# Spectral mixing with three complex products in place of four, an inverse transform in 64-row tiles, and part of the weight conversion on GpSimd

## The chip, the cores and the metric

The kernel runs on one core of a Trainium2 chip. The metric is the device time of one execution in microseconds (us). The engines have short names: PE is TensorE (PEld its weight loads), DVE is VectorE, ACT is ScalarE, POOL is GpSimd, and SP is SyncE, which issues nearly all transfers.

## The reference

A spectral layer is followed by two MLPs. B is 2, S 3008, D 256, the hidden width 2048.

```python
X = np.fft.rfft(x, axis=1)
Yr = Xr @ w_r - Xi @ w_i + b_r
Yi = Xr @ w_i + Xi @ w_r + b_i
Yr = np.sign(Yr) * np.maximum(np.abs(Yr) - 0.01, 0.0)      # the same for Yi
y = np.fft.irfft(Yr + 1j * Yi, n=S, axis=1)
h = y @ w_in;  g = np.maximum(h, 0) + alpha * np.minimum(h, 0);  y = g @ w_out
h = y @ w_in2; g = np.where(h >= 1, h, np.where(h <= -1, 0, (h + 1)**2 / 4)); out = g @ w_out2
```

The MLP weights are float64 and come to the chip as pairs of 32-bit words.

## The kernel before

The program is written in order by hand: each engine works through its instructions in the order of the code, and semaphores tie them together.

1. **First transform.** `f1(g)`, 16 groups: four products of 256 columns each, whose results are written to memory (`store_a`) and read back in another layout (`load_a` into `a_sb`).
2. **Mixing loop.** 24 items `(b, i)`, 12 for each batch entry. `f2` makes the spectrum of an item with four products of 128 columns. ACT and DVE split it into a high part `xh` and a low part `xl` with the imaginary part negated beside it. `mix` multiplies by the two weight matrices `wm`: each output half takes six kinds of products (high and low of the data with high and low of the weights) over two halves of the depth, 24 products of 256 columns in all. DVE adds the bias and shrinks (`y32`). `i1` is the first step of the inverse transform, two float32 products of 256 columns. In round `j` of the loop stand `f2` of item j+2, `mix` of item j and `i1` of item j-2.
3. **Conversion of the first MLP's weights.** `conversions` is a generator that turns 16 blocks (`f`) of word pairs into a high and a low part. Each block takes four steps: `begin_w` (ACT) with the previous block's `fraction_w`; `words_w` (ACT, DVE) with the previous block's `high_w` (ACT); `low_w`; then `clamp_w` and `sign_w`. The mixing loop and the MLP loop each advance it by some steps in every round. When it has ended, the MLP loop advances `second_weights`, the second MLP's weights, in the same way.
4. **Second inverse step** `p3`, with operands of 48 rows in 64-row halves and results of 64 rows, run in pairs (`p3_two`) in rounds 17, 19 and 21.
5. **The MLPs.** `trio` takes 48 steps, with `first` and `second` of six products of 512 columns each, then further chunks and pairs of chunks.

Where PE waits for a bank of its result memory (PSUM), the bank's tag tells who holds it: `e` and `h` have two buffers each, `o0` to `o3` one each.

Of the kernel before, what the change touches and what calls it, by code (L numbers as in the profile page):

```python
# [31 lines left out]
def fourier_constants():  # L32
# [21 lines left out]
    for k in range(NK):  # L54
# [39 lines left out]
def spectral_mlp_kernel(ctx: ExitStack, tc: tile.TileContext, x, w_r, w_i, bias, c_f1, c_f2,  # L94
# [55 lines left out]


# [33 lines left out]
    def clamp_w(m):  # L185
        V.tensor_scalar(m, m, W_MAX, W_MIN, op0=ALU.min, op1=ALU.max)

    def conversions(l, fs):
# [5 lines left out]
        for k in range(n + 1):  # L194
# [139 lines left out]
    ps = psum.tile([128, 256], F32, tag="h", name="ps_warm")
    for _ in range(3):
        T.matmul(ps, warm[:, 0:128], warm, start=True, stop=True)


    c47 = base.tile([96, 96], F32, name="c47")
# [87 lines left out]
    wm = [block(f"c{k}", [128, 2, 2, D], F32R, f"wm{k}") for k in range(2)]  # L427
    held = []
    for g in range(8, 16):
        f1(g, held if g == 15 else None)  # L430
        if g < 15:
            store_a(g, 0)
        if g in (13, 14):

            hi, lo = (wm[g - 13][:, z].rearrange("p c (h q) -> p c q h", h=2) for z in range(2))
# [579 lines left out]
```

## Time and profile before

| | us |
|---|---|
| median of 3 runs (1104.27 to 1104.53) | 1104.45 |
| the profiled execution | 1104.76 |
| its span in the profile | 1103.0 |
| PE, DVE, ACT, POOL busy | 1094.4, 914.4, 863.6, 0.2 |
| mixing loop, from its first product to the second MLP step | 34.85 to 150.18 |
| the 48 `trio` steps, about | 146 to 269 |

Busy time of PE is a model of pipelined products, so the pace of PE is read from the starts of its instructions, not from how long each is said to take. Start times are us from the start of the span. A product of two float32 operands shows as two records, one of two float32r operands as one.

### The profile page before, as it was taken

The page shows a single profiled execution, that of the slowest core. Times are in us where ns is not written, and L with a number is a line of the kernel's source. Part 1 is how long each engine was busy: PE and PEld are TensorE (multiplying, and loading weights), DVE is VectorE, ACT ScalarE, POOL GpSimd, SP SyncE. Part 2 cuts the span into 40 slices and gives each one's busy share as a digit, 9 for nine tenths or more (in the row PEclk, how much of TensorE's full clock was granted, in tenths as well). Part 3 has the DMA queues.
Part 4 walks back from the last instruction along what each step waited for, and adds up shares of the span by engine and source line. Part 5 has one row for each costly group of instructions (what it writes and reads, how often), then busy time and mean ns, then how long its engine had stood idle before and what let it go on. Part 6 is the DMA issues. An engine that isn't in the chain of part 4 may idle for free.

```text
span 1103.0 us, 17331 instructions
## 1 busy us (share of the span) xinstructions
PE 1094.4 (99%) x6416; PEld 969.4 (88%) x6416; DVE 914.4 (83%) x1578; ACT 863.6 (78%) x1636; POOL 0.2 (0%) x4
## 2 busy tenths in 40 slices
PE   9999999999999999999999999999999999999998
PEld 7999988888888998888889988888899888888897
DVE  3579968888778989999999999877878878878876
ACT  3555678878777889999989978877778878877876
POOL 0000000000000000000000000000000000000000
PEclk9999999999999999999999999999999999999999
DMA  9997663101322403323235623010010000100101
GB/s 288 305 285 252 185 168 82 32 1 58 111 101 96 153 21 115 115 81 111 96 136 189 218 107 135 1 39 1 1 39 1 37 1 1 39 1 1 39 1 37
DMA packets 50004, 101.34 MB, mean 92 GB/s; under 512 B 5024, under 2 KB 27392, under 8 KB 49920
## 3 DMA queue, kind: packets, MB, share of 16 engines
q1 hardware_dynamic: 49664, 100.08, 27.8%
q8 instruction: 51, 0.84, 0.3%
q14 instruction: 33, 0.27, 0.1%
q10 hardware_dynamic: 256, 0.16, 0.0%
HBM read 64.70 MB, written 35.52 MB: 91 GB/s over the span
## 4 chain that ended last, share of the span: by engine, by line
PE 83%; ACT 8%; DVE 7%; issue 2%; ACTq 0%; DVEq 0%
PE pq L114 9%; PE pq L115 9%; PE pq L113 9%; PE psm L467 6%; PE seeded L113 3%; PE psh L113 3%; PE psh L115 3%; PE psh L114 3%; PE pso L113 3%; PE pso L114 3%; PE seeded L114 3%; PE seeded L115 3%; PE pso L115 3%; PE ps L387 3%; PE psA L113 2%; PE psA L115 2%
## 5 line engine op out<-in xcount | busy, mean ns | idle before, releaser
L113 PE MATMUL pq<-gh,w 128*128 128x512 f32 (+1 forms) x576 | 216.7, 376 | 0.8 <-ACT yt L802 0.4
L114 PE MATMUL pq<-gl,w 128*128 128x512 f32 (+1 forms) x576 | 216.5, 376 | 0.8 <-DVE gl L773 0.6
L115 PE MATMUL pq<-gh,w 128*128 128x512 f32 (+1 forms) x576 | 215.8, 375 | 0.0
L770 ACT ACTIVATE gh<-ta 128x512 fp32r<-128x512 f32 (+1 forms) x144 | 88.6, 627 | 90.8 <-DVE ta L767 86.0
L113 PEld LDWEIGHTS pq<-gh,w 128*128 128x128 f32 x576 | 108.8, 189 | 16.3 <-ACT yt L802 2.1
L114 PEld LDWEIGHTS pq<-gl,w 128*128 128x128 f32 x576 | 108.8, 189 | 15.6 <-DVE gl L773 2.8
L115 PEld LDWEIGHTS pq<-gh,w 128*128 128x128 f32 x576 | 108.9, 189 | 12.7
L773 DVE TENSOR_TENSOR gl<-tb,gh 128x512 fp32r<-128x512 f32 (+1 forms) x96 | 65.3, 680 | 55.9 <-ACT gh L770 55.6
L773 DVE TENSOR_TENSOR gl<-ta,gh 128x512 fp32r<-128x512 f32 (+1 forms) x144 | 97.5, 677 | 3.9 <-ACT gh L770 2.0
L110 DVE TENSOR_TENSOR gl<-ta,gh 128x512 fp32r<-128x512 f32 (+1 forms) x96 | 65.1, 678 | 42.8 <-ACT gh L107 42.6
L578 ACT ACTIVATE ta<-psh 128x512 f32<-128x512 f32 (+1 forms) x96 | 56.7, 591 | 50.2 <-DVE gl L110 32.7
L861 DVE TENSOR_TENSOR h<-psC,s 128x512 f32<-128x512 f32 (+1 forms) x72 | 48.9, 680 | 29.7 <-PE psC L115 25.9
L113 PE MATMUL psh<-mxh,w 128*128 128x512 f32 (+1 forms) x192 | 72.4, 377 | 0.5 <-ACT tb L579 0.5
L114 PE MATMUL pso<-gl,w 128*128 128x512 f32 (+1 forms) x192 | 72.4, 377 | 0.0
L113 PE MATMUL pso<-gh,w 128*128 128x512 f32 (+1 forms) x192 | 72.3, 377 | 0.0
L114 PE MATMUL psh<-mxl,w 128*128 128x512 f32 (+1 forms) x192 | 71.9, 375 | 0.0
L115 PE MATMUL pso<-gh,w 128*128 128x512 f32 (+1 forms) x192 | 71.9, 375 | 0.0
L115 PE MATMUL psh<-mxh,w 128*128 128x512 f32 (+1 forms) x192 | 71.9, 375 | 0.0
L581 DVE SCALAR_TENSOR_TENSOR ta<-ta,nalpha,tb 128x512 f32<-128x512 f32 (+1 forms) x96 | 70.5, 734 | 0.0
L767 DVE SCALAR_TENSOR_TENSOR tb<-tb,h 128x512 f32<-128x512 f32 (+1 forms) x96 | 60.6, 673 | 0.0
L107 ACT ACTIVATE gh<-ta 128x512 fp32r<-128x512 f32 (+1 forms) x96 | 60.2, 628 | 0.3 <-DVE ta L581 0.3
L770 ACT ACTIVATE gh<-tb 128x512 fp32r<-128x512 f32 (+1 forms) x96 | 59.2, 617 | 1.6 <-DVE tb L767 1.6
(141 smaller groups left out, 2723.4 us busy)
## 6 DMA issues: line engine op xcount, KB each, us to landing
s<-kept SPq DMA_DIRECT2D x32, 512.0 KB, 4.0
u<-in_w_in SPq DMA_DIRECT2D x32, 256.0 KB, 3.6
u<-in_w_out SPq DMA_DIRECT2D x32, 256.0 KB, 3.7
kept<-sh SPq DMA_DIRECT2D x16, 512.0 KB, 2.9
kept<-wh SPq DMA_DIRECT2D x16, 512.0 KB, 3.0
w<-kept SPq DMA_DIRECT2D x16, 512.0 KB, 4.7
v_dr<-ve SPq DMA_DIRECT2D x12, 512.0 KB, 3.6
v<-v_dr SPq DMA_DIRECT2D x32, 192.0 KB, 5.1
```

Of the source, the lines that this page charges most:

```text
L107: A.activation(hi, src, AF.Copy)
L110: V.tensor_tensor(lo, src, hi.bitcast(F32), op=ALU.subtract)
L113: T.matmul(ps, wl, xh, start=start, stop=False, skip_group_check=chained)
L114: T.matmul(ps, wh, xl, start=False, stop=False, skip_group_check=chained)
L115: T.matmul(ps, wh, xh, start=False, stop=stop, skip_group_check=chained)
L467: T.matmul(o, x[:, 2 * k + c, off:off + 128], wm[r][:, z, c, :].rearrange("p (h q) -> p q h", h=2), start=n == c == 0, stop=n == 5 and c == 1)
L578: A.activation(ta, ps, AF.Relu, scale=-1.0)
L581: V.scalar_tensor_tensor(ta, ta, nalpha[:, f:f + 1], tb, op0=ALU.mult, op1=ALU.add)
L767: V.scalar_tensor_tensor(self.t, self.t, 1.0, self.h, op0=ALU.min, op1=ALU.max)
L770: A.activation(halves(self.gh, self.m), like_halves(self.t, self.m), AF.Copy)
L773: V.tensor_tensor(halves(self.gl, self.m), like_halves(self.t, self.m), halves(self.gh, self.m).bitcast(F32), op=ALU.subtract)
L861: V.tensor_tensor(blk.h, ps[x], ps[y_], op=ALU.add)
```

## The change

- The complex product uses three real ones. `f2` lays its result out as real, imaginary and their sum; `mix_sum` multiplies the sum by `w_r`, DVE adds the bias and writes the result twice into one of two fixed banks (`ri`), and `mix` lets PE add two further products to what stands there. Each of the three takes six products of 256 columns (high by low, high by high, low by high over two halves of the depth). `wm` holds `w_r`, `-(w_r + w_i)` and `w_i - w_r`.
- The shrinking is an ACT `Relu` and one DVE instruction.
- `i1` takes four products with 64 rows of depth in place of two with 128; even and odd ones use the lower and the upper rows and write different banks.
- For `f < 7`, `clamp_w`, the product in `fraction_w` and both instructions of `low_w` run on GpSimd.
- In the loops, rounds 5 to 22 advance the conversion by 1 or 2 steps in turn (2 before, with 2 more in round 17); `trio` advances it by 1 step from step 2 on and by 2 in every third step below 38 (1 before, from step 5, none in every eighth).
- At the start, the last two groups of the first transform stand behind the first `f2`, and their inputs are loaded behind the first `load_a`. `p3` runs singly in rounds 16 to 21.

```diff
@@ conversion
+    NG = 7
+    def side(f):
+        return G if f < NG else V
...
         V.tensor_scalar(p.bitcast(U32), m.bitcast(U32), 0xFF800000, None, op0=ALU.bitwise_and)
-        V.tensor_tensor(p, p, u[:, :, 0].bitcast(F32), op=ALU.mult)
+        side(f).tensor_tensor(p, p, u[:, :, 0].bitcast(F32), op=ALU.mult)
...
-        V.tensor_tensor(m, m, wt[l, f][:, 0, :].bitcast(F32), op=ALU.subtract)
-        V.tensor_tensor(wt[l, f][:, 1, :], m, p, op=ALU.add)
+        side(f).tensor_tensor(m, m, wt[l, f][:, 0, :].bitcast(F32), op=ALU.subtract)
+        side(f).tensor_tensor(wt[l, f][:, 1, :], m, p, op=ALU.add)
...
-                clamp_w(live[l, fs[k]][1])
+                clamp_w(live[l, fs[k]][1], side(fs[k]))
@@ start
     for g in range(8):
         f1(g)
         store_a(g, 0)
-        load_x(8 + g)
+        if g < 6:
+            load_x(8 + g)
...
     load_a(0, A_PARTS[:2])
+    load_x(14)
+    load_x(15)
...
+        if g == 12:
+            split_wm(0, wm32[0])
+            ws = [rot.tile([128, 2, D], F32, tag=t, name=f"ws{t}") for t in ("cm", "cp")]
+            V.scalar_tensor_tensor(ws[0], wm32[0], -1.0, wm32[1], op0=ALU.mult, op1=ALU.subtract)
+            V.tensor_tensor(ws[1], wm32[1], wm32[0], op=ALU.subtract)
+            split_wm(1, ws[0])
+        if g == 13:
+            split_wm(2, ws[1])
+    for k in range(2):
+        f2(*items[k], **(dict(tag="e") if k else dict(tag="o3", bufs=1)))
+        f1(14 + k)
+        store_a(14 + k, 0)
+    mix_sum(*items[0])
@@ f2
-        A.activation(xh[:, :, 64:192], ps, AF.Copy)
-        A.mul(xh[:, :, 0:64], ps[:, :, 64:128], -1.0)
-        V.tensor_tensor(xl[:, :, 64:192], ps, xh[:, :, 64:192].bitcast(F32), op=ALU.subtract)
-        A.mul(xl[:, :, 0:64], xl[:, :, 128:192].bitcast(F32), -1.0)
+        A.activation(xi, ps[:, 256:512], AF.Copy)
+        V.tensor_tensor(s32, ps[:, 0:256], xi, op=ALU.add)
+        A.activation(xh[:, 0:512], ps, AF.Copy)
+        A.activation(xh[:, 512:768], s32, AF.Copy)
+        V.tensor_tensor(xl[:, 0:512], ps, xh[:, 0:512].bitcast(F32), op=ALU.subtract)
+        V.tensor_tensor(xl[:, 512:768], s32, xh[:, 512:768].bitcast(F32), op=ALU.subtract)
@@ mix
+    def product3(o, x, t, w, start):
+        o = o.rearrange("p (q h) -> p q h", h=2)
+        for n, (z, v) in enumerate(((0, 1), (0, 0), (1, 0))):
+            for c in range(2):
+                T.matmul(o, x[z][:, t, c, :], w[:, v, c, :].rearrange("p (h q) -> p q h", h=2),
+                         start=start and n == c == 0, stop=n == 2 and c == 1, skip_group_check=not start)
...
+    def mix_sum(b, i):
+        ps = psum.tile([128, 1, D], F32, tag="o2", bufs=1, name=f"psk{b}_{i}")
+        product3(ps[:, 0, :], xt[b, i], 2, wm[0], True)
+        V.tensor_tensor(ri[i % 2], ps.to_broadcast([128, 2, D]), b_t, op=ALU.add)
...
-            for n, (r, x, z) in enumerate(((0, xh, 1), (0, xh, 0), (1, xh, 1), (1, xh, 0), (0, xl, 0), (1, xl, 0))):
-                for c in range(2):
-                    off = 0 if r else 64
-                    T.matmul(o, x[:, 2 * k + c, off:off + 128], wm[r][:, z, c, :].rearrange("p (h q) -> p q h", h=2),
-                             start=n == c == 0, stop=n == 5 and c == 1)
...
-        V.tensor_tensor(t, ps, b_t.to_broadcast([128, 2, D]), op=ALU.add)
-        V.tensor_scalar(cl_, t, LAM, -LAM, op0=ALU.min, op1=ALU.max)
-        V.tensor_tensor(y32, t, cl_, op=ALU.subtract)
+        x, y = xt.pop((b, i)), ri[i % 2]
+        for z in range(2):
+            product3(y[:, z, :], x, 1 - z, wm[1 + z], False)
+        A.activation(t, y, AF.Relu, bias=-LAM)
+        V.scalar_tensor_tensor(y32, y, LAM, t, op0=ALU.add, op1=ALU.min)
@@ i1
-        for k in range(2):
-            T.matmul(ps[:, k, :], n_t[i // 4][:, (2 * i + k) % 8, :], y32[:, k, :], start=True, stop=True)
+        for z in range(2):
+            for k in range(2):
+                rows = slice(64 * k, 64 * k + 64)
+                n = 2 * (i % 4) + z
+                T.matmul(ps[k], n_t[i // 4][rows, n, :], y32[rows, z, :], start=z == 0, stop=z == 1)
...
-        A.activation(ve[b][:, 2 * (i % 2):2 * (i % 2) + 2, :], ps, AF.Copy)
+        for k in range(2):
+            A.activation(ve[b][:, 2 * (i % 2) + k, :], ps[k], AF.Copy)
@@ loops
-        if 0 < j < n - 2:
+        if j < n - 2:
             f2(*items[j + 2])
+        if j + 1 < n:
+            mix_sum(*items[j + 1])
         mix(*items[j])
...
-        if j in (17, 19, 21):
-            p3_two(j - 17)
+        if 16 <= j < 22:
+            p3(j - 16)
...
-        for _ in range(j == 2 or (2 if 5 <= j < n - 1 else 0) + (2 if j == 17 else 0)):
+        for _ in range(j == 2 or (1 + j % 2 if 5 <= j < n - 1 else 0)):
             next(conv)
...
-        if 5 <= i < len(trio) and i % 8 != 0 and next(conv, more) is more:
-            next(more, None)
+        if 2 <= i < len(trio):
+            for _ in range(1 + (i % 3 == 0 and i < 38)):
+                if next(conv, more) is more:
+                    next(more, None)
```

PE in one round of the mixing loop, before: `psf` is written by `f2`, `psm` by `mix`, `psi` by `i1`; `fh` and `fl` are `xh` and `xl`.

```order
L447 MATMUL psf_9_693<-m_102,a_210 128x128 x4
L467 MATMUL psm_7_704<-wm_237,fh_7_581 128x256 x4
L467 MATMUL psm_7_704<-wm_238,fh_7_581 128x256 x4
L467 MATMUL psm_7_704<-wm_237,fl_7_582 128x256 x2
L467 MATMUL psm_7_704<-wm_238,fl_7_582 128x256 x2
...
L481 MATMUL psi_5_735<-y_0_5_614,n_104 128x256 x2
```

The same place of the changed kernel; `psk` is written by `mix_sum`, and `ri` by `mix`.

```order
L440 MATMUL psf_8_645<-m_102,a_204 128x2x64 x4
L461 MATMUL psk_7_659<-wm_235,fh_7_592 128x256 x4
L461 MATMUL psk_7_659<-wm_235,fl_7_593 128x256 x2
L461 MATMUL ri_77<-wm_236,fh_6_545 128x256 x4
L461 MATMUL ri_77<-wm_236,fl_6_546 128x256 x2
L461 MATMUL ri_77<-wm_237,fh_6_545 128x256 x4
L461 MATMUL ri_77<-wm_237,fl_6_546 128x256 x2
L514 MATMUL psi_4_0_683<-y_0_4_575,n_104 128x256
L514 MATMUL psi_4_1_684<-y_0_4_575,n_104 128x256
L514 MATMUL psi_4_0_683<-y_0_4_575,n_104 128x256
L514 MATMUL psi_4_1_684<-y_0_4_575,n_104 128x256
```

Of the 24 products for `psm` (the left-out rows are the second output half), 18 are left, six of them for the item that follows, and `i1` has four products where it had two.

ACT in one round of the mixing loop in which the conversion stands, before: `ve` is what `i1` gave, `cm`, `u` and `w` belong to the conversion, and the rows behind them are the next item's.

```order
L484 ACTIVATE ve_6_794<-psi_7_845 128x512
L162 ACTIVATE u_2_631<-u_2_631 128x512
L183 ACTIVATE w_1_856<-cm_1_690 128x512
L452 ACTIVATE fh_0_868<-psf_0_863 128x4x128
L453 ACTIVATE fh_0_868<-psf_0_863 128x4x64
L455 ACTIVATE fl_0_869<-fl_0_869 128x4x64
```

ACT in round 7 of the changed kernel; `t` is the `Relu`, and `s` the copy of the imaginary part or the sum beside it.

```order
L501 ACTIVATE t_7_733<-ri_78 128x512
L518 ACTIVATE ve_4_689<-psi_5_0_737 128x256
L518 ACTIVATE ve_4_689<-psi_5_1_738 128x256
L163 ACTIVATE cm_1_748<-u_1_482 128x512
L168 ACTIVATE u_1_482<-u_1_482 128x512
L189 ACTIVATE w_0_753<-cm_0_637 128x512
L448 ACTIVATE s_0_10_765<-psf_10_758 128x256
L450 ACTIVATE fh_10_763<-psf_10_758 128x512
L451 ACTIVATE fh_10_763<-s_0_10_765 128x256
```

An item has six instructions on ACT where it had four, and in such a round three of the conversion's stand ahead of the next item's first.

PE at the start of the mixing loop, before; `ps_1_7` is the last group of the first transform.

```order
L387 MATMUL ps_1_7_0_309<-x_7_206,c_81 96x256 x2
L387 MATMUL ps_1_7_1_312<-x_7_206,c_81 96x256 x2
L447 MATMUL psf_315<-m_100,a_210 128x128 x4
L447 MATMUL psf_329<-m_100,a_210 128x128 x4
L467 MATMUL psm_0_340<-wm_237,fh_0_320 128x256 x4
```

The same in the changed kernel:

```order
L440 MATMUL psf_0_305<-m_100,a_204 128x2x64 x4
L393 MATMUL ps_1_6_0_319<-x_6_207,c_81 96x256 x2
L393 MATMUL ps_1_6_1_323<-x_6_207,c_81 96x256 x2
L440 MATMUL psf_1_328<-m_100,a_204 128x2x64 x4
L393 MATMUL ps_1_7_0_342<-x_7_209,c_81 96x256 x2
L393 MATMUL ps_1_7_1_346<-x_7_209,c_81 96x256 x2
L461 MATMUL psk_0_351<-wm_235,fh_0_310 128x256 x4
```

Two groups of the first transform moved behind the first `f2`.

## Rows read from the trace of the kernel before

**Rows 1.** The page's first part: busy us, share of the span, instructions.

```profile
PE 1094.4 (99%) x6416; PEld 969.4 (88%) x6416; DVE 914.4 (83%) x1578; ACT 863.6 (78%) x1636; POOL 0.2 (0%) x4
```

**Rows 2.** Timeline, PE, one round of mixing: start, us, engine, line, operation.

```profile
47.10 1.05 PE L447 MATMUL psf<-m,a 128*128 128x128 f32 x8
47.91 1.14 PE L467 MATMUL psm<-wm,fh 128*128 128x256 f32 x8
...
50.67 1.03 PE L481 MATMUL psi<-y,n 128*128 128x256 f32 x4
...
51.54 1.05 PE L447 MATMUL psf<-m,a 128*128 128x128 f32 x8
```

**Rows 3.** Stretches: length, busy PE, PEld, DVE, ACT, POOL, PEclk, DMA share, GB/s.

```profile
46.89:77.90 31.01, 31.01 (x253) 30.31 (x252) 22.43 (x39) 15.34 (x32) 0.00 (x0) 1.00 0.92 302
90.00:100.00 10.00, 10.00 (x82) 9.74 (x82) 9.63 (x19) 6.32 (x14) 0.00 (x0) 1.00 0.52 188
156.00:270.00 114.00, 114.00 (x530) 99.82 (x529) 95.46 (x162) 88.74 (x161) 0.00 (x0) 1.00 0.22 54
```

**Rows 4.** Timeline, PE, around a `p3_two` (L549) in the mixing loop.

```profile
112.78 1.03 PE L481 MATMUL psi<-y,n 128*128 128x256 f32 x4
113.74 2.09 PE L549 MATMUL ps<-g,v 48*64 48x47 f32 x128
115.77 1.16 PE L447 MATMUL psf<-m,a 128*128 128x128 f32 x8
116.68 1.14 PE L467 MATMUL psm<-wm,fh 128*128 128x256 f32 x8
```

**Rows 5.** Groups, 0 to 330 us: busy us, mean ns; idle before, releaser.

```profile
L454 DVE TENSOR_TENSOR fl<-psf,fh 128x512 fp32r<-128x512 f32 x24 | 16.5, 687 | 7.5 <-ACT fh L453 7.5
L452 ACT ACTIVATE fh<-psf 128x512 fp32r<-128x512 f32 x24 | 14.3, 597 | 2.0 <-PE psf L447 2.0
L453 ACT ACTIVATE fh<-psf 128x256 fp32r<-128x256 f32 x24 | 9.3, 388 | 0.0
L266 DVE TENSOR_TENSOR sh<-w 128x256 f32<-128x256 f32 x16 | 6.0, 418 | 0.0
```

**Rows 6.** The same view: the conversion's instructions, one of each for a block.

```profile
L162 ACT ACTIVATE u<-u 128x512 f32<-128x512 uint32 x16 | 13.5, 845 | 0.0
L157 ACT ACTIVATE cm<-u 128x512 f32<-128x512 f32 x16 | 13.1, 818 | 4.3 <-DMA u<-in_w_out 2.8 <-DVE w L179 1.5
L174 DVE TENSOR_TENSOR cp<-cp,u 128x512 f32<-128x512 f32 x16 | 12.4, 773 | 0.6
L168 DVE SCALAR_TENSOR_TENSOR cm<-cm,cp 128x512 uint32<-128x512 uint32 x16 | 11.1, 692 | 0.5
L179 DVE TENSOR_TENSOR w<-cm,cp 128x512 fp32r<-128x512 f32 x16 | 11.1, 692 | 0.5
L178 DVE TENSOR_TENSOR cm<-cm,w 128x512 f32<-128x512 f32 x16 | 11.0, 688 | 1.7 <-ACT w L183 1.6
L183 ACT ACTIVATE w<-cm 128x512 fp32r<-128x512 f32 x16 | 10.2, 640 | 0.1
L163 DVE TENSOR_SCALAR cp<-u 128x512 uint32<-128x512 uint32 x16 | 7.5, 468 | 0.0
L173 DVE TENSOR_SCALAR cp<-cm 128x512 uint32<-128x512 uint32 x16 | 6.8, 424 | 0.3
L186 DVE TENSOR_SCALAR cm<-cm 128x512 f32<-128x512 f32 x16 | 6.7, 420 | 0.0
```

**Rows 7.** Timeline: the first `f2`'s weight load; the second `load_a`; `f2` of item 12.

```profile
33.01 1.86 PEld L447 LDWEIGHTS psf<-m,a 128*128 128x128 f32 x16 [0.16 <-DMA a<-a_dr]
...
71.10 0.82 SPq L361 DMA_DIRECT2D a<-a_dr  x2
...
78.16 1.05 PE L447 MATMUL psf<-m,a 128*128 128x128 f32 x8
```

**Rows 8.** Transfers by line, the `load_a` parts of 256 KB: median us to landing.

```profile
a<-a_dr SPq DMA_DIRECT2D x8, 256.0 KB, 4.2
```

More of the change, by code (lines that the diff above doesn't have):

```diff
@@ L183, in high_w, with clamp_w @@
         A.activation(wt[l, f][:, 0, :], m, AF.Copy)
-    def clamp_w(m):
-        V.tensor_scalar(m, m, W_MAX, W_MIN, op0=ALU.min, op1=ALU.max)
+    def clamp_w(m, engine=V):
+        engine.tensor_scalar(m, m, W_MAX, W_MIN, op0=ALU.min, op1=ALU.max)
     def conversions(l, fs):
@@ L322, in second_weights @@
         yield
-    turn = [0]
+    turn = [2]
     def obank(shape, name, ahead=None):
@@ L330, in obank @@
         return psum.tile(shape, F32, tag=f"o{k}", bufs=1, name=name)
-    warm = rot.tile([128, 256], F32, tag="ta", name="warm")
+    warm = rot.tile([128, 512], F32, tag="ta", name="warm")
     V.memset(warm, 0.0)
[L334 to L339, printed above, removed]
+    ri = [psum.tile([128, 2, D], F32, tag=f"o{k}", bufs=1, name=f"ri{k}") for k in range(2)]
+    for k in range(2):
+        T.matmul(ri[k].rearrange("p z e -> p (z e)"), warm[:, 0:128], warm, start=True, stop=True)
+    c47 = block("small", [128, 128], F32, "c47")[0:96, 0:96]
     A.dma_start(c47, c_f1)
@@ L426, in spectral_mlp_kernel, with f2 @@
     next(conv)
[L427 to L435, printed above, removed]
-            split(wm32[g - 13].rearrange("p c (q h) -> p c q h", h=2), hi, lo, A)
     items = [(b, i) for b in range(B) for i in range(NK // 2)]
     xt, y_32, ve = {}, {}, {}
-    def f2(b, i, ps=None):
-        if ps is None:
-            ps = psum.tile([128, 4, 128], F32, tag="h", name=f"psf{b}_{i}")
+    def f2(b, i, **where):
+        ps = psum.tile([128, 2, 2, 2, R2], F32, **(where or {"tag": "h"}), name=f"psf{b}_{i}")
         for k in range(2):
             for c in range(2):
-                T.matmul(ps[:, 2 * k + c, :], a_sb[b][:, 2 * i + k, c * 128:(c + 1) * 128],
+                T.matmul(ps[:, :, c, k, :], a_sb[b][:, 2 * i + k, c * 128:(c + 1) * 128],
                          m_t[i // 4][:, (2 * i + k) % 8, :], start=True, stop=True)
@@ new lines, in mix_sum, with split_wm @@
+    def mix_sum(b, i):
+        ps = psum.tile([128, 1, D], F32, tag="o2", bufs=1, name=f"psk{b}_{i}")
+        product3(ps[:, 0, :], xt[b, i], 2, wm[0], True)
+        V.tensor_tensor(ri[i % 2], ps.to_broadcast([128, 2, D]), b_t, op=ALU.add)
+    def split_wm(k, w):
+        hi, lo = (wm[k][:, z].rearrange("p c (h q) -> p c q h", h=2) for z in range(2))
+        split(w.rearrange("p c (q h) -> p c q h", h=2), hi, lo, A)
+    for g in range(8, 14):
+        f1(g)
+        store_a(g, 0)
+        if g == 12:
[6 more added lines that the diff above has]
+            split_wm(2, ws[1])
@@ L605, in p3_two @@
                 load_v(k)
-    for j in range(2):
-        f2(*items[j], obank([128, 4, 128], f"psf_{j}", 2 + j))
-        if j == 0:
-            for (dst, ps), copy in zip(held, (lambda d, p: A.activation(d, p, AF.Copy), V.tensor_copy)):
-                copy(dst, ps)
-            store_a(15, 0)
     for j in range(n):
-        if 0 < j < n - 2:
+        if j < n - 2:
             f2(*items[j + 2])
+        if j + 1 < n:
+            mix_sum(*items[j + 1])
         mix(*items[j])
-        if j == 0:
-            f2(*items[2])
         if j >= 2:
```

42 lines of the change are left out of this document (22 added, 20 removed).

## The prediction

> **What bounds the kernel now.** I read the busy times first: PE is busy for 99% of the span, DVE for 83%, ACT for 78%, and GpSimd does nothing [rows 1]. Since PE's busy time is a model, I checked it in the timeline of one round of the mixing loop [rows 2]. `f2` starts at 47.10, `mix` at 47.91, `i1` at 50.67 and the next `f2` at 51.54. So a round takes 4.44 us, made of 0.81 for `f2`, 2.76 for `mix` and 0.87 for `i1`, and one part starts where the last one's work ends. The 24 products of `mix` take 2.76 / 24 = 0.115 us each. The stretches say the same: 82 PE records in 10 us, and 253 in 31 [rows 3], are the 36 records of a round every 4.4 us. PE sets the pace, and what is taken from its queue is won unless another engine becomes late. The one that is near is DVE: 9.63 us of 10 while the conversion stands beside the mixing, with ACT at 6.32 [rows 3]. In the MLP steps PE issues 530 records in 114 us, 2.58 us for a step of twelve, with DVE at 95.46 of 114 us, or 2.16 a step, and ACT at 88.74, or 2.01 [rows 3]. The granted clock is 1.00 in all these stretches.
>
> **Mixing: what goes.** Six of 24 products leave each item: 6 x 0.115 = 0.69 us, and over 24 items 16.6 us.
>
> **Mixing: `i1` in row halves.** It has four products where it had two, each with the same 256 columns. If the lower and the upper rows work side by side it still takes 0.87 us; one after the other it takes 1.74. No row shows this shape. The nearest is `p3_two`, which uses 64-row halves and results of 64 rows: 128 records of 47 columns between 113.74 and 115.77, 15.9 ns each [rows 4]. `f2` takes 0.81 / 8 = 101 ns for a record of 128 columns [rows 2], so 47 columns alone would take 37 ns. `p3_two` is 2.3 times as fast. The two halves of its result can give at most a factor of 2, so at least 1.17 comes from the row halves. That bounds `i1` between 0.87 and 1.74 / 1.17 = 1.49 us. I take 0.87: at 15.9 ns for a load and a product `p3_two` may be held by issuing alone, and `i1` has 109 ns for each of its eight records.
>
> **Mixing: the seams.** Going from full height to halves costs something. From `i1` to `p3_two` it is 112.78 to 113.74, 0.96 where `i1` takes 0.87; the `f2` behind it takes 115.77 to 116.68, 0.91 for 0.81 [rows 4]. That is 0.19 us for both seams, paid once for each item now: 24 x 0.19 = 4.6 us. The lower bound is nothing, should the seams hide behind loads. `p3` run singly borders on `i1`, so its seams about cancel against those of the three pairs it replaces. A round is then 4.44 - 0.69 + 0.19 = 3.94 us.
>
> **DVE and ACT in the mixing.** DVE's item is a sum and a split of 256 columns (0.418 each), a split of 512 (0.687), the bias and the shrinking (like that split): 2.90 us [rows 5]. A block's conversion costs DVE 4.16 us in seven instructions, of which the four that move to GpSimd are 0.420 + 0.773 + 0.688 + 0.692 = 2.57 and the three that stay 1.58 [rows 6]. At 1.5 of four steps a round that is 0.59, so DVE needs 3.49 of 3.94 us. The 28 conversion steps of the loop reach just through the seven blocks that GpSimd serves. ACT's item is three copies of 256 columns at 0.388 (the imaginary part and two halves of `i1`'s result), one more for the sum, and two instructions of 512 at 0.597, the `Relu` among them: 2.75 us [rows 5]. A block's three ACT instructions are 0.845 + 0.818 + 0.640 = 2.30 [rows 6], so ACT needs 2.75 + 0.86 = 3.61 of 3.94, up from 63% to 92%. On average both fit. In single rounds they don't: in rounds 7 and 15 all three conversion instructions stand in front of the next item's first copy, in round 5 two (1.66), in rounds 10 and 13 two (1.49). What is queued behind them is the chain imaginary copy, split, copy of the sum, low part, bias (0.39 + 0.60 + 0.39 + 0.42 + 0.69 = 2.49). It begins 0.78 after the round's start, when `i1`'s copies are done, and has to end when the next `mix_sum` wants bank `o2`, 3.94 + 0.81 = 4.75 after it. The room is 1.48 us. Rounds 5, 7 and 15 exceed it by 0.18, 0.82 and 0.82, 1.8 in all; if the hand-overs between engines take 0.5 of it, the sum with rounds 10 and 13 is 4.3. I take 3.0; rounds 16 to 21 have `p3`'s 1.0 us as cover. Lower bound 0, if the pieces one item ahead absorb it.
>
> **GpSimd.** Its 28 instructions are costed at nothing, because `clamp_w` waits only on ACT's first instruction and `low_w` only on ACT's high part, both given a round or so earlier, and a block has 2.7 rounds, 10 us. No row shows GpSimd arithmetic; the price without cover stands under the rivals.
>
> **The start.** Before, the first `f2` waited 0.16 us for `load_a` at 33.01 [rows 7], so transfer and PE arrive together. Now PE comes there two groups of the first transform earlier, 8 products of 256 columns or 4 x 0.87 = 3.5 us. The transfer gets ahead by two input groups of 393 KB, which at 302 GB/s [rows 3] is 2.6 us. So some 0.9 us of waiting is new. DVE also has a third split and two sums of the mixing weights, 2 us and more, in front of the first item. I take 1.5 us of loss, from 0 to 3.5.
>
> **Item 12.** The next batch entry's `load_a` is issued at 71.10 [rows 7] and lands 4.2 us later [rows 8], at 75.3; transfers fill 0.92 of the time until then [rows 3], so I don't expect it sooner. Its `f2` stood at 78.16 [rows 7]. Now ten rounds give back 6.9, eight pairs of seams take 1.5, the start 1.5 and rounds 5 and 7 some 1.5: 75.8. No wait is added, but the loop can't be over 2.9 us ahead there, which caps the gain.
>
> **MLP steps.** The loop leaves 39 conversion steps to `trio` where it left 28, and nine more steps of the second weights come forward: 20 steps at 4.16 / 4 = 1.04, the conversion's price for both, are 20.8 us of DVE over 48 steps, 0.43 each. DVE goes from 2.16 to 2.59 us against PE's 2.58: full, not yet over. ACT goes to about 2.25. I take 1.0 us, from 0 to 3.
>
> **Sum.** -16.6 + 4.6 + 3.0 + 1.5 + 1.0 = -6.5 us. From the profiled execution's 1104.76 that gives 1098.3; the median stands 0.3 below it, so 1098.0.
>
> **Rivals.** *Row halves one after the other (slower).* `i1` then takes 0.87 us more, 24 x 0.87 = 20.9, of which the 3.0 for ACT would be hidden: 1098 + 17.9 = 1116. It turns slower than before from 0.4 us an item on. Against it speaks the factor of 2.3 [rows 4]; for it, that only 1.17 of it is proved for rows.
>
> *GpSimd holds up DVE.* If each of the 28 instructions stopped DVE for as long as DVE itself takes for one (0.69 [rows 6]), DVE would lose 19.3 us in rounds 5 to 22. Its room there is 18 x 0.45 and 6 x 1.0 of `p3`, 14; the other 5 come back to PE: 1103, no change. It would be slower from about 0.8 us a stop on. Rows can't decide it, but most of DVE's instructions in the mixing read one operand from PSUM, and many will not meet GpSimd.
>
> The Trainium skill has a rule for this ("SBUF — State Buffer", section "SBUF: two separate sides"): VectorE and GpSimd share a port pair by an exclusive lock held for a whole instruction, and VectorE needs it in its 2-port modes or with two SBUF inputs. Its "GPSIMD Engine Reference" (section 3.1) gives about 2.6 cycles at 1.2 GHz for each element of a two-input instruction, so I estimate 1.1 us for one of ours. If every one were a stop, 31 us, the time by these pages would be near 1115. No row of this trace shows GpSimd working, so it stays a rival.
>
> *The items' chain sets the pace.* If the chain over ACT and DVE holds all rounds near 4.3 us instead of 3.94, 24 x 0.36 = 8.6 are gone instead of the 3.0: 1103.6, no change. For it: ACT at 92%.
>
> *More than forecast.* Seams hidden and no burst felt: 2.9 us by item 12 and 14 x 0.69 = 9.7 behind it: 1092.
>
> **How the numbers follow.** The measurement tells 0.2%, 2.2 us, from no change. The forecast (1094.5 to 1102) gets 0.60, more than it 0.15, rows in turn 0.06, GpSimd 0.11 (half of it slower), the chain 0.05, others on the slow side 0.03. So faster 0.76, same 0.10, slower 0.14. The range runs from 1092, the capped best case, to 1105, which leaves out the slow cases.
>
> **What would show it.** The round on PE falls from 4.44 to near 3.94 us, with `i1` at 0.87 plus seams; `i1` at 1.5 or more proves the first rival. PE waits on the bias or on the low parts in rounds 7 and 15. GpSimd's instructions should stand beside DVE's without stretching them. In the MLP steps 2.58 us a step shows that DVE still keeps up. The forecast fails if a step's new cost on DVE or ACT shows as PE idle over several rounds.

## The result and the profile after

The changed kernel takes 1120.1 us (median of 4 runs, 1119.43 to 1121.5), the kernel before beside it 1104.49. The ratio is 1.0142, with a 95% interval of 1.0124 to 1.0159: slower by 1.4%, where 1098.0 was forecast and the range ended at 1105. The profiled execution took 1121.5 us, its span 1119.3.

The page's first part of the changed kernel, which answers to [rows 1]:

```profile
PE 1096.9 (98%) x6366; PEld 953.6 (85%) x6366; DVE 911.1 (81%) x1577; ACT 884.1 (79%) x1685; POOL 33.5 (3%) x32
```

PE is not busy for less time than before, though it has 144 products less, and the span is 16.3 us longer. So time went in idle stretches and in slow ones. Where, shows when the same work is reached. Five marks divide the span: `f2` of item 4 on PE (the mixing loop at `j` = 2), and ACT's `tb<-psh`, its second copy of a step's `first`, of the MLP steps 0, 48 (the first behind `trio`), 60 and 95. The table gives the time to the first mark and from each to the next, from the starts of these rows, for every run below. All later comparisons come from it.

| run | to item 4 | mixing | `trio` | steps 48 to 60 | steps 60 to 95 | rest |
|---|---|---|---|---|---|---|
| before | 42.7 | 105.5 | 123.3 | 35.5 | 93.9 | 702.1 |
| after | 52.8 | 102.8 | 129.5 | 41.4 | 92.9 | 700.0 |
| e1_start | 51.8 | 103.2 | 129.6 | 41.2 | 92.8 | 700.0 |
| e2_even | 50.4 | 103.3 | 132.4 | 35.7 | 93.6 | 702.0 |
| e3_dve | 50.8 | 105.9 | 129.1 | 41.4 | 92.9 | 699.9 |
| e5_three | 51.5 | 101.8 | 131.3 | 35.1 | 94.0 | 702.4 |
| e6_loads | 48.1 | 103.2 | 129.6 | 41.2 | 92.9 | 700.0 |
| e7_sched | 50.3 | 108.7 | 124.7 | 35.5 | 94.0 | 702.0 |
| e8_two | 49.3 | 110.0 | 124.7 | 35.6 | 93.8 | 702.0 |
| e9_rows | 50.8 | 112.0 | 130.0 | 41.3 | 93.0 | 700.0 |
| e10_mend | 49.9 | 101.8 | 131.2 | 35.2 | 93.9 | 702.0 |
| e11_mend_gp | 48.1 | 101.8 | 141.6 | 35.9 | 93.6 | 702.1 |
| e12_thin_after | 51.4 | 100.2 | 126.3 | 41.3 | 92.7 | 699.9 |
| e13_thin_before | 41.7 | 105.6 | 123.3 | 35.5 | 93.9 | 701.9 |
| e14_hold | 49.9 | 103.3 | 129.1 | 36.1 | 92.9 | 701.9 |
| e15_best | 50.3 | 101.8 | 129.0 | 35.3 | 93.7 | 701.9 |
| e16_early | 47.9 | 103.8 | 126.8 | 35.9 | 93.5 | 701.9 |
| e17_oneweight | 47.4 | 101.7 | 131.2 | 35.2 | 93.8 | 702.0 |

The first two lines are the result in short. The start lost 10.1 us, the mixing gave back 2.7, `trio` lost 6.2, the next twelve MLP steps 5.9; the rest gave back 3.1. Runs whose code for the start is the same (after, e2, e3, e7, e9, e12, e14) reach item 4 between 49.9 and 52.8, with a mean of 50.9, so this column holds to some 3 us, and the profile of after is at its late end. The other columns repeat far better.

**The start.** The timeline of the changed kernel (start, us, engine or queue, line, operation, idle before and its releaser):

```profile
19.23 0.39 SPq L414 DMA_DIRECT2D wm<-in_w_r  x1
...
23.23 1.08 SPq L371 DMA_DIRECT2D a_dr<-ae  x2
...
28.94 1.94 PE L393 MATMUL ps<-x,c 96*96 96x256 f32 x8 [0.35 <-DMA x<-in_x]
...
30.52 0.82 SPq L367 DMA_DIRECT2D a<-a_dr  x2
...
31.38 0.90 SPq L357 DMA_DIRECT2D x<-in_x  x2
...
33.27 1.13 PE L440 MATMUL psf<-m,a 128*128 128x128 f32 x8 [2.38 <-DMA a<-a_dr]
...
38.04 3.70 PE L393 MATMUL ps<-x,c 96*96 96x256 f32 x8 [3.63 <-DMA x<-in_x]
```

And stretches (length, busy PE, PEld, DVE, ACT, POOL, PEclk, DMA share, GB/s):

```profile
28.00:34.00 6.00, 3.27 (x17) 2.15 (x16) 4.74 (x7) 3.85 (x5) 0.00 (x0) 1.00 0.62 194
34.00:38.00 4.00, 0.40 (x4) 0.21 (x2) 2.20 (x4) 1.28 (x3) 0.00 (x0) 0.53 0.95 237
38.00:42.00 4.00, 3.96 (x11) 2.90 (x12) 0.23 (x1) 0.59 (x1) 0.00 (x0) 0.50 1.06 371
42.00:46.00 4.00, 4.00 (x19) 3.33 (x19) 1.90 (x5) 1.76 (x4) 0.00 (x0) 0.69 1.01 353
46.00:50.00 4.00, 3.96 (x36) 3.80 (x36) 2.71 (x7) 1.65 (x4) 0.00 (x0) 1.00 0.76 247
```

`load_a` is issued at 30.52, later than the kernel before's 29.88, because it waits for stores to land (its longest wait for one is 5.9 us, where it was 3.2); the change also put the mixing weights' loads ahead of the last of these stores. So the first `f2` stands at 33.27, where it stood at 33.11 before, but two groups of the first transform are still to be done. Their inputs are queued behind `load_a`. So PE waits for `a`, then for `x`, and is busy for 3.67 of the 10 us from 28 to 38. The granted clock then stands at 0.50 to 0.53, the 1.2 GHz level, and comes back to 1.00 by 46: the 8 records of 38.04 show 3.70 us where the same ones at 28.94 show 1.94.

**A round of mixing.** PE's timeline, which answers to [rows 2]:

```profile
61.32 1.16 PE L440 MATMUL psf<-m,a 128*128 128x128 f32 x8
62.24 0.69 PE L461 MATMUL psk<-wm,fh 128*128 128x256 f32 x4
...
64.42 1.14 PE L514 MATMUL psi<-y,n 64*128 64x256 f32 x8
65.48 1.16 PE L440 MATMUL psf<-m,a 128*128 128x128 f32 x8
```

A round takes 4.16 us: 0.92 for `f2`, 2.18 for the 18 products, 1.06 for `i1`. Forecast was 3.94. In rounds 8, 9, 12 and 15 the starts of `f2` lie 4.7 to 5.0 apart; with most of the conversion left out (e12) each of them takes 4.16. What PE waits for from 50 to 157 us (in total, times, the longest):

```profile
PE psk L461 <- DVE ri L470: 1.5, 4, 0.6
PE psf L440 <- DVE fl L452: 0.5, 1, 0.5
```

**The last item.** The `i1` of item 23 stands between the MLP steps 0 and 1, behind a `p3`. PE there, before and then after:

```profile
149.43 1.13 PE L481 MATMUL psi<-y,n 128*128 128x256 f32 x4
150.21 0.57 PE L113 MATMUL psh<-mxh,w 128*128 128x512 f32 x1
```

```profile
156.98 0.70 PE L514 MATMUL psi<-y,n 64*128 64x256 f32 x2
158.00 1.13 PE L514 MATMUL psi<-y,n 64*128 64x256 f32 x6 [0.33 <-ACT yt L587]
159.06 0.48 PE L114 MATMUL psh<-mxh,w 128*128 128x512 f32 x1
```

It takes 2.08 us in place of 0.78: its six later records begin at 158.00, when ACT has copied results of `p3` (`yt`). Between the marks of steps 0 and 1 every run with half-height `i1` falls back 1.40 us (1.44 in e11), whatever its conversion does; this lies in the `trio` column.

**The MLP steps.** Stretches that answer to [rows 3]:

```profile
90.00:100.00 10.00, 9.67 (x80) 8.40 (x80) 7.01 (x13) 6.88 (x17) 4.01 (x4) 1.00 0.88 304
156.00:270.00 114.00, 112.01 (x576) 93.59 (x569) 103.31 (x179) 91.33 (x165) 4.99 (x3) 1.00 0.30 79
```

DVE is busy for 103.31 of 114 us, where it was 95.46. The timeline of DVE, POOL and PE near 170 us:

```profile
168.51 1.64 POOL L184 TENSOR_TENSOR cm<-cm,w 128x512 f32<-128x512 f32 x1 [0.72 <-ACT w L189]
168.92 1.60 DVE L169 TENSOR_SCALAR cp<-u 128x512 uint32<-128x512 uint32 x1
170.22 2.05 POOL L185 TENSOR_TENSOR w<-cm,cp 128x512 fp32r<-128x512 f32 x1
...
171.06 1.76 DVE L615 SCALAR_TENSOR_TENSOR ta<-ta,small,tb 128x512 f32<-128x512 f32 x1
...
175.67 0.48 PE L115 MATMUL pso<-gl,w 128*128 128x512 f32 x1 [1.64 <-DVE gl L111]
```

Beside GpSimd a DVE instruction of 0.47 [rows 6] takes 1.60 and one that takes 0.75 in the median takes 1.76; 4 us later PE waits 1.64 for `gl`. That GpSimd stretches them, e3 shows, which has no arithmetic there: these two groups take at most 0.53 and 0.77. The same holds for the low part of the sum in the mixing (shortest, median and longest ns), after and then e3:

```profile
L453 DVE TENSOR_TENSOR fl<-s,fh x24: 415/415/1239, 36.6 to 144.1; 128x256 fp32r<-128x256 f32 x24
```

```profile
L453 DVE TENSOR_TENSOR fl<-s,fh x24: 412/415/417, 36.3 to 144.3; 128x256 fp32r<-128x256 f32 x24
```

Behind `trio`, in the timeline of the queue and of ACT:

```profile
293.55 0.47 SPq L149 DMA_DIRECT2D u<-in_w_out  x1
...
297.37 0.88 ACT L242 ACTIVATE wh<-u 128x512 f32<-128x512 f32 x1 [3.23 <-DMA u<-in_w_out]
```

ACT stands for 3.23 us at the second weights' first operation, since its input was issued at 293.55; the MLP steps' copies queue behind it.

### The profile page after: what moved, and what is told of

It is laid out like the page before. It is cut to its first block, busy times and chain, and to the rows that moved or that the text cites. A ratio compares the mean times of both kernels' runs of the same rounds, so it can differ in the third digit from the quotient of the medians.

```text
span 1119.3 us, 17375 instructions
## 1 busy us (share of the span) xinstructions
PE 1096.9 (98%) x6366; PEld 953.6 (85%) x6366; DVE 911.1 (81%) x1577; ACT 884.1 (79%) x1685; POOL 33.5 (3%) x32
## 4 chain that ended last, share of the span: by engine, by line
PE 65%; DVE 10%; ACT 9%; issue 2%; DMA 0%; SPq 0%; ACTq 0%; DVEq 0%
PE pq L115 10%; PE pq L114 10%; PE pq L116 10%; PE seeded L114 4%; PE seeded L116 4%; PE seeded L115 4%; PE psA L114 3%; PE psA L116 2%; PE psA L115 2%; PE psC L116 2%; DVE gl L111 2%; PE psC L115 2%; PE psC L114 2%; PE psh L114 2%; PE pso L115 2%
## 5 line engine op out<-in xcount | busy, mean ns | idle before, releaser
L114 PEld LDWEIGHTS pq<-gh,w 128*128 128x128 f32 x576 | 108.8, 189 | 16.3 <-ACT yt L834 2.6
L615 DVE SCALAR_TENSOR_TENSOR ta<-ta,small,tb 128x512 f32<-128x512 f32 (+1 forms) x96 | 71.5, 745 | 0.0
L791 ACT ACTIVATE ta<-ta 128x512 f32<-128x512 f32 (+1 forms) x96 | 59.3, 617 | 1.5
```

Source lines behind the costliest of these rows:

```text
L114: T.matmul(ps, wl, xh, start=start, stop=False, skip_group_check=chained)
L615: V.scalar_tensor_tensor(ta, ta, nalpha[:, f:f + 1], tb, op0=ALU.mult, op1=ALU.add)
L791: A.activation(self.t, self.t, AF.Square)
```

## The experiments

**Three parts mended one by one.** e1 put the start into the order of the kernel before: all sixteen groups loaded, then the mixing weights, and all groups transformed ahead of the first `f2`. Its core:

```diff
-        if g < 6:
-            load_x(8 + g)
+        load_x(8 + g)
...
-    for g in range(8, 14):
+    for g in range(8, 16):
```

> The start alone is put back into the old order: all 16 input groups are loaded without a pause, the mixing weights are loaded behind them, all eight second-half groups are transformed before the first items' second step, and the first items' transfer is issued behind the mixing weights. Theory (the new order of the start costs the 10 us by which the second step of item 4 lies later in the changed kernel, 52.78 against 42.66): that step begins by 44.5 and the time falls from 1120.1 to 1110 to 1112 us. Rival (the three weight splits and sums on ScalarE and VectorE, or a clock that stays low, cost most of it, not the order): the step stays at 47 or later and the time at 1115 or above.

It took 1120.73 us (1.0138, 1.0123 to 1.0154), and item 4 came at 51.8. The theory fell, but not to its rival alone. The waits for `a` and `x` were gone and a new one stood in their place:

```profile
32.47 1.09 ACT L108 ACTIVATE wm<-wm 128x512 fp32r<-128x512 f32 x1 [4.41 <-DMA wm<-in_w_r]
...
36.79 2.95 PEld L393 LDWEIGHTS ps<-x,c 96*96 96x96 f32 x8 [5.48 <-ACT ae_late L395]
```

The first weight split stood in ACT's order ahead of two evictions, and now came before its input had landed; PE waited 5.48 us for those evictions.

e2 thinned the conversion in `trio`:

```diff
-            for _ in range(1 + (i % 3 == 0 and i < 38)):
+            for _ in range(1 + (i % 12 == 0 and i < 38)):
```

> Only the schedule of the weight conversion in the trio stage is thinned: two conversion steps in one MLP step come every twelfth step in place of every third. Theory (the denser schedule costs the 9.5 us that the trio and the later chunks lie behind: VectorE stands at 9.9 of 10 us from 170 to 240, and the second weights reach their DMA-fed step early): the lag at the pair step behind the trio shrinks from 12.6 to about 9.5, that at the last output eviction from 18.4 to 13 or less, and the time is 1111 to 1114 us. Rival (the stretched VectorE work beside GpSimd, or the late start itself, costs it): 1118 to 1121.

1119.87 (1.0116 to 1.0146), so the rival's time; but the table shows a trade. Steps 48 to 60 got their 5.7 us back. `trio` lost 2.9 more, since weights came late: PE's waits there name the conversion's last instruction.

```profile
PE psh L114 <- DVE w L185: 2.6, 2, 2.2
```

e3 set `NG = 0`:

> The arithmetic of all weights' conversion goes back to VectorE, the rest of the changed kernel stays. Theory (GpSimd's 33.5 us are worth about what they take from VectorE, since instructions of VectorE beside them are stretched two- to threefold): 1118 to 1125 us, nearly no change. Rival A (GpSimd holds up VectorE and that is what the trio loses): 1110 to 1114. Rival B (the relief of VectorE is real, it is the bound from 170 to 240): 1128 or above.

1121.37 (1.0127 to 1.0161): the theory's no change. GpSimd is worth 3.1 us in the mixing loop and costs 0.4 in `trio`.

e5 joined e1, e2 and mixing steps spread as `"112121121121222221"` over rounds 5 to 22:

> The start in the old order, the thinner schedule of the conversion, and in the mixing rounds the 27 steps of the background work spread so that no round before the inverse-transform rounds has two of ScalarE's steps in a row. Theory (the three losses are separate and add: 10 us of the start, some 8 of the schedule, 3 of the rounds): 1098 to 1102 us, faster than the kernel before (1104.5). Rival (the losses cover one another, or the first items' next transfer holds the earlier rounds up): 1106 to 1112.

1117.45 (1.0097 to 1.0128): both numbers were missed. Steps 48 to 60 were mended and the mixing gained 1.0; start and `trio` kept their losses.

**Second repairs.** e6 loads all inputs early and transforms all sixteen groups ahead of the first `f2`, with one weight split behind each of groups 12, 13, 14, and with the first shared product (`mix_sum` of item 0) behind the third item's `f2`. Of its edit:

```diff
-    for g in range(8, 14):
+    for g in range(8, 16):
...
-        if g == 13:
+        if g == 14:
             split_wm(2, ws[1])
```

> A second repair of the start: the last two input groups are loaded with the others, ahead of the items' transfer; the eight second-half groups are transformed without a pause; one weight split stands behind each of groups 12, 13 and 14, so that ScalarE has its input landed when it comes to it (in the run with the old order of loads ScalarE waited 4.41 us for the mixing weight in front of two evictions, and TensorE 5.48 us behind it); and the first shared product stands behind the third item's second step. Theory (the start is lost in two waits, for the late input groups and in front of evictions, and in the half clock that follows the idle time; take both waits away and it comes back): idle time of TensorE between 28 and 40 falls from about 8.8 to 3 us or less, the granted clock stays at 1.00, and the time falls to 1111 to 1114 us. Rival (the transfer of the first items sets the second step at 33.2 and all behind it whatever the order is): 1117 or above.

1118.78 (1.0114 to 1.0148). PE is busy through 34, but the waits moved on, and the clock still fell to 0.57 from 38 to 42:

```profile
37.97 1.76 PE L437 MATMUL psf<-m,a 128*128 128x128 f32 x8 [2.11 <-DVE fl L449]
...
43.11 0.68 PE L458 MATMUL psk<-wm,fh 128*128 128x256 f32 x4 [2.10 <-DVE ri L467]
```

The time is the rival's, its reason is not: item 4 at 48.1 is 4.7 earlier than in after, 2.8 earlier than the mean of the seven runs with after's start, and other waits hold it there.

e7 put back only the conversion's schedule (2 steps a round, 2 more in round 17; in `trio` 7 of 8), e8 both it and e6's start:

> Only the schedule of the weights' conversion is as in the kernel before: two steps in every mixing round from the sixth, two more in round 17, and one step in seven of eight MLP steps of the trio; the rest is the changed kernel. Theory (the change moved some ten steps, about 10 us of VectorE's time, from the mixing rounds into the trio, where VectorE had 8.4 of 10 already; that and the earlier second weights cost 9 to 10 us): the lag grows by no more than 2 between the trio's first step and the output's last eviction (11.0 in the changed kernel), the mixing rounds get 2 to 4 us longer in all, and the time is 1112 to 1115 us. Rival (the rounds of 4.16 can't take two steps, and lose what the trio gains): 1118 to 1121.

> Both: the second repair of the start and the schedule of the kernel before. Theory (two separate losses that add): 1103 to 1108 us, at the kernel before's 1104.5 or near it. Rival (the losses cover one another): 1112 or above.

1117.2 (1.0102 to 1.0132), between its two accounts, and 1117.77 (1.0103 to 1.0133), the rival. `trio` and the steps behind it stand within 1.4 us of the kernel before, but the mixing loop takes 108.7 and 110.0, 3.2 and 4.5 more than there. In e7 the rounds 7 to 15, with two steps each, take about 4.27 or 4.55, some 2 us over 4.16 in all. The larger part stands behind the four steps of round 17: rounds 18 and 19 take 8.37 and 6.87, where after and e16 (two steps in round 17) have 5.24 for each. The timeline of e7:

```profile
127.37 0.69 DVE L174 SCALAR_TENSOR_TENSOR cm<-cm,cp 128x512 uint32<-128x512 uint32 x1 [5.12 <-POOL cm L192]
...
130.27 1.97 PE L440 MATMUL psf<-m,a 128*128 128x128 f32 x8 [3.06 <-DVE fl L452]
```

With four steps of a block in one round DVE comes to an instruction whose input GpSimd still works on, and the item's low part waits behind it. So most of what e7 loses in the mixing is this burst and not two steps a round, which e16 below has in nearly every round.

e9 measures the row halves. Its `i1` uses all 128 rows for the same four products:

```diff
-                T.matmul(ps[k], n_t[i // 4][rows, n, :], y32[rows, z, :], start=z == 0, stop=z == 1)
+                T.matmul(ps[k], n_t[i // 4][:, n, :], y32[:, z, :], start=z == 0, stop=z == 1)
```

> The inverse transform's four products of an item take all 128 rows in place of two halves of 64 (each output then holds the sum over both halves, so the values differ from the reference; the count of products and everything around them stays). Theory (a float32 product is two records in order, so that halves overlap only between neighbours and eight records take five slots of 0.217 us, more than four full products in 0.87): the round falls from 4.16 to 3.94 to 4.00 and the time from 1120.1 to 1115 to 1117 us. Rival (halves are as fast as full products and the round's last fifth of a us is a seam at a change of tile): round 4.16, time 1119 to 1121.

The time rose to 1129.4 (1.0211 to 1.0241), which neither account gave. The theory's 0.87 was misread: in [rows 2] that is two products, four records. PE's timeline:

```profile
65.03 1.05 PE L440 MATMUL psf<-m,a 128*128 128x128 f32 x8
65.84 0.69 PE L461 MATMUL psk<-wm,fh 128*128 128x256 f32 x4
...
67.93 1.89 PE L513 MATMUL psi<-y,n 128*128 128x256 f32 x8
69.66 0.61 PE L440 MATMUL psf<-m,a 128*128 128x128 f32 x4
```

Eight full records take 1.73 us, 0.216 each, eight half-height ones 1.06. Halves save 0.67 where full overlap would save 0.87. Without them `f2` and the products take 0.81 and 2.09, so the seams cost 0.92 + 2.18 - 0.81 - 2.09 = 0.20 us a round.

**Is it the conversion?** e10 repairs the start a third time (`f2` of item 0 between groups 14 and 15, the third split behind group 15), with e2's and e5's schedules; e11 adds `NG = 16`. e12 and e13 leave out most of the first layer's conversion, in the changed kernel and in the kernel before: `words_w`, `sign_w`, `fraction_w`, the clamp and one of `low_w`'s instructions.

> A third repair of the start (the last two input groups loaded with the others; group 14 transformed ahead of the first item's second step, group 15 between those of the first two items, the third weight split behind it), with the thinner schedule of the trio and the spread steps of the mixing rounds. What earlier runs showed is put together: start 8 to 10 behind, of which the second repair took 4 to 5 back; thinner schedule and spread steps took the chunks' 5 back but left 8 to 9 in the trio. Theory (VectorE and ScalarE have no room in the shorter rounds, so that conversion costs time wherever it is put): item 4's second step at 47 to 48, the trio still 7 to 9 behind, time 1110 to 1114 us. Rival (only places were wrong): 1104 or below.

> The kernel of the run with the third repair, with the arithmetic of all sixteen weights on GpSimd in place of seven. Theory (room on VectorE is what the trio lacks; nine more weights take some 2.5 us each off it there, and give part of that back where instructions lie beside GpSimd's): the trio's lag falls by 3 to 5 us, time 3 to 5 us under that run. Rival (what lies beside GpSimd is stretched as much as is relieved): within 1 us of it, or slower.

> The changed kernel without most of the first layer's weight conversion: of a weight's arithmetic only the first ScalarE operation, the copy to the high half and one subtraction stay (VectorE 0.69 in place of some 4.1 us of arithmetic a weight, GpSimd none; the weights' values differ). Theory (the losses in the rounds, the trio and the chunks, 3 and 6 and 5 us, are conversion that no longer fits beside the shorter rounds): the time falls by 9 to 14 us to 1106 to 1111, with the start's loss left. Rival (the conversion has nothing to do with it; the lag comes from the second weights, the transfers or the clock): 1116 or above.

> The kernel before with the same thinning of the first layer's weight conversion. Theory (there the conversion is hidden: TensorE has no idle time in the mixing rounds or the trio): 1103 to 1105 us, no change from 1104.5, so that the distance between the two kernels falls from 15.6 to 2 to 7 us. Rival (conversion costs time in the kernel before too): it falls by 3 us or more.

e10: 1117.95 (1.0096 to 1.0132), neither; item 4 came at 49.9. e11: 1127.29 (1.0188 to 1.0227), 9.3 slower than e10, the rival. PE's waits in `trio`:

```profile
PE pso L115 <- DVE gl L111: 6.7, 8, 1.0
PE psh L114 <- POOL w L185: 4.8, 2, 3.1
```

GpSimd delivers weights too late, and `gl` on DVE is late as well. e13 took 1104.29, ratio 1.0 (0.999 to 1.0009), so the kernel before hides its conversion wholly. e12 took 1113.62 (1.0057 to 1.0089), between its two accounts, 2.6 above the theory's. Its mixing loop takes 100.2 against e13's 105.6, a saving of 5.4 us, and after's conversion costs 2.6 of that. In `trio` 3.0 stay lost, 1.4 of it at the last item's `i1`, and steps 48 to 60 still take 41.3. Its conversion, cheap as it is, is still stepped twice in places, and there ACT meets a load that has not landed:

```profile
ACT cm L162 <- DMA u<-in_w_out: 2.9, 1, 2.9
```

**What was still open:** whether the early second weights alone cost the steps behind `trio`, what the third mixing weight costs at the start, and where conversion is cheapest. e14 changes one line of after; e15 is e10 with after's rate and that line; e16 takes 35 steps in the rounds and one a step in `trio`; e17 is e10 with one mixing weight for all three.

```diff
-                if next(conv, more) is more:
+                if next(conv, more) is more and i >= 38:
```

> The changed kernel; only the second weights' steps in the trio are held back to the last ten MLP steps, as many as the kernel before has there (the changed kernel has nineteen). Theory (nine steps too early bring the second weights' first operation right behind its own loads, and ScalarE waits there with the MLP's operations behind it): the lag that grows by 5 from MLP step 48 to 60 of the trace's row on tb stays flat, within 1, and the time falls by 4 to 6 us to 1114 to 1116. Rival (the later chunks lose to the late start of their transfers): the lag grows by 3 or more there, and the time stays above 1118.

> The third repair of the start, the spread steps of the mixing rounds, the changed kernel's conversion rate in the trio, and the second weights held back. Theory (what each took back adds: start 5.5, spread 1, chunks 5): lag 3 to 4 at the trio's first step, 8 to 10 behind it, flat from there, time 1108 to 1112 us. Rival (conversion makes up whatever the start gains, as in the run with the third repair): 1115 or above.

> As the run before in this list, but with two conversion steps in nearly every mixing round (35 in place of 27) and one in each MLP step of the trio. Theory (a step in a round of 4.16 costs about 0.25 us, a step too many in the trio some 0.6): rounds 2 us longer in all, trio 3 to 5 us shorter, time 1 to 3 us under that run. Rival (ScalarE and VectorE are as full in the rounds as in the trio): equal within 1 us, or slower.

> The kernel of the run with the third repair of the start, with one mixing weight in place of three (its split serves all three products, the two sums and two splits are left out, so the values differ). Theory (what is left of the start's loss is work of ScalarE and VectorE that three products added: two splits of 2.2 us, sums of 1.3 us, a shared product's sum with the bias 0.69, in order in VectorE's queue ahead of the first items): the wait for the first sum with the bias falls from 3.0 to under 1.5, item 4's second step begins 2 to 3 us earlier, near 44.5, and the time falls 2 to 3 us from 1118.0. Rival (the chain of the first items itself, five operations that alternate between ScalarE and VectorE, sets it): item 4 within 1 us of 47.0.

e14: 1116.14 (1.009 to 1.0122), 4.0 less than after, with steps 48 to 60 in 36.1 us: the theory. Stretches of after and of e14 at the same place:

```profile
300.00:310.00 10.00, 8.06 (x37) 6.43 (x36) 7.24 (x13) 7.78 (x16) 0.00 (x0) 1.00 0.00 0
```

```profile
300.00:310.00 10.00, 10.00 (x166) 8.70 (x165) 9.19 (x18) 8.08 (x17) 0.00 (x0) 1.00 0.22 85
```

e15: 1113.81 (1.0064 to 1.0094), between theory and rival; e16: 1112.24 (1.0053 to 1.0087), 1.6 under it, within what the theory gave: the mixing 2.0 longer as expected, `trio` 2.2 shorter where 3 to 5 were, the start 2.4 earlier with the same code. It is the fastest of these and still behind the kernel before. e17: 1113.63 (1.0067 to 1.0097). Its expectation took item 3's start in e10, 47.0, for item 4's; item 3 moved to 44.5 and item 4 from 49.9 to 47.4, 2.6 each, and the waits for `ri` from 3.0 to 1.4. PE's waits from 26 to 60 us, of e10 and then of e17:

```profile
PE psk L458 <- DVE ri L467: 3.0, 1, 3.0
```

```profile
PE psk L458 <- DVE ri L467: 1.4, 1, 1.4
```

The time fell by 4.3, more than the theory gave. But e16, with e10's start, also reached item 4 at 47.9, so 2.6 lies within this column's spread; the shorter wait is the better evidence, since it is 2.0 to 3.0 us in the four runs with e10's start (e10, e11, e15, e16).

## Why the prediction was wrong, point by point

By the columns of the table the forecast is 9.6 us too low at the start (1.5, less 1.0 for the two rounds that lie there, against 10.1), 5.3 in the mixing (8.0 to be gained in 22 rounds, 2.7 gained) and 8.0 behind it (1.0 against 6.2 + 5.9 - 3.1). The times that two rivals gave, 1116 and 1115, lie nearer to 1120.1, but not for their reasons: `i1` is not doubled, and without GpSimd (e3) the time is no shorter.

- **PE sets the pace:** right. e13 shows it from the other side: with most of the conversion gone, the kernel before is no faster.
- **Six products less, 16.6 us:** right. The 18 products take 2.09 us where no seam is beside them (e9), 0.116 each.
- **Seams, 0.19:** right, 0.20.
- **`i1` in halves at 0.87:** mis-sized; it takes 1.06, inside the bounds of 0.87 to 1.49. That is 24 x 0.19 = 4.6 us, and together with the seams the round is 4.16. Without bursts the mixing's gain was 24 x 0.28 = 6.7 us, not 12.0 (from item 4 on, e12 against e13: 5.4). The 1.4 us at the last item were in no term.
- **Bursts on ACT, 3.0:** the size was right, 2.6 (mixing of after less that of e12), and PE waits for the bias and a low part, as it said. They lie in rounds 8, 9, 12 and 15 in place of 5, 7 and 15. That ACT's bursts alone make them is not shown: e12 takes DVE's and GpSimd's work away too, and e3 shows that DVE's matters there.
- **GpSimd at nothing:** not quite. e3 and e11 show a gain where DVE has gaps and a loss where it is full, and e7 a wait of 5.12 us where a block's steps come too close together. The Trainium skill ("SBUF — State Buffer", section "SBUF: two separate sides") has VectorE and GpSimd share a port pair by an exclusive lock; the stretched rows at 168.92 and 171.06 agree. As the sole cause of the loss it falls, since e3 without GpSimd was no faster.
- **The start, 1.5:** the step that failed first. It took the transfer to "get ahead by two input groups"; `load_a` waits for stores to land and was issued no earlier, and the price of a late group, PE idle and then at half clock, was not in the sum. It is 7.2 to 10.1 us. Against the mean of 50.9, the first repair of the order (e1, e5) reached item 4 at 51.8 and 51.5, the second (e6, e8) at 48.1 and 49.3, the third (e10, e11, e15, e16) at 47.9 to 50.3. Each met the next wait: splits in front of evictions, then the low part and the bias on DVE in front of the first items, which e17 shortens with one weight. So several late things stand in a chain, of which e1, e6 and e17 each show one; no run here recovered the start wholly, and how its loss divides among them is open.
- **MLP steps, 1.0:** the second step that failed. It summed busy time (2.59 against PE's 2.58) and left out what an instruction waits for in its engine's order. `trio` lost 6.2 and steps 48 to 60 another 5.9, of which 3.1 came back behind them. That the latter come from nine second-weight steps too early is shown by one line (e14, with 4.0 us less in time); the wait of 3.23 for a load that has not landed is the largest single one there. In `trio`, 1.4 belong to the last item's `i1`. The other 4.8 are the conversion's schedule: in e7, with the old schedule, `trio` loses the 1.4 and nothing behind step 1; in e16, with fewer steps left for `trio`, 2.1 are left beside the 1.4; in e12 1.6 remain without DVE's work, beside a conversion that outruns its loads. How 4.8 divides between DVE's queue, GpSimd's stretching and such waits was not separated.
- **Item 12, 0:** right but idle, since the loop never got ahead; its `f2` stood at 87.84.

What joins the two failures is a trade that the sum missed. The new mixing takes 0.69 us a round from PE and puts 0.4 us on DVE and 0.7 on ACT: 2.90 and 2.75 an item, where it was 0.69 + 0.43 + 0.69 + 0.69 and 0.60 + 0.39 + 0.42 + 0.60. The conversion, hidden in rounds of 4.44, no longer hides wholly at 4.16: moved into `trio` it costs there, kept in the rounds it costs there (e16 with 35 steps takes 2.0 us more in the mixing than e10 with 27). Mixing and `trio` together take 228.8 us before, 232.3 after, 230.6 in the best order found, and 226.5 without the conversion.

## What to carry to other kernels

Before taking work off the engine that sets the pace, list what hides behind it: here 5.4 us gained on PE uncovered a conversion that had cost nothing (e13). A step placed on an in-order engine costs what it waits for, its loads above all, so a schedule made denser must be checked against landing times, and not only against busy shares. An input moved behind a transfer that itself waits for stores is late by that wait, and the idle time that it makes is paid again in clock.

## What the runs showed of the hardware

- Eight half-height float32 records on alternating row halves take 1.06 us, eight full ones 1.73. That is about five slots of 0.216, which would fit if a product's two records stay in order and only neighbouring products overlap; this reading was not isolated.
- Behind PE's idle time of 28 to 38 us the granted clock stood at 0.50 to 0.53, and products of one shape took 3.70 us in place of 1.94.
- GpSimd's float32 two-input instruction on 128x512 takes a mean of 1.33 to 1.39 us, where the prediction estimated 1.1, and DVE's beside it took 1.60 and 1.76 where they take 0.47 and 0.75 alone (at most 0.53 and 0.77 in e3):

```profile
L185 POOL TENSOR_TENSOR w<-cm,cp 128x512 fp32r<-128x512 f32 x7 | 9.7, 1385 | 0.5
L184 POOL TENSOR_TENSOR cm<-cm,w 128x512 f32<-128x512 f32 x7 | 9.3, 1327 | 19.0 <-ACT w L189 19.0
```
